# One-bank PSUM tiles for the last up projection of a fused attention and feed-forward kernel

## The chip, the cores and the metric

The kernel runs on one core of a Trainium2 chip. A core has TensorE (PE, matrix products, with a loader PEld for the stationary operand), VectorE (DVE), ScalarE (ACT), GpSimd (POOL) and the queue engine SyncE (SP). PSUM, where TensorE writes, is used here as eight banks of 128 partitions x 512 float32 values. The metric is the device time of one execution in microseconds (us); several runs are made, and the profile shows one execution.

## The reference

Two stages. A chunked linear attention with a decay per head, over 4 batches, 8 heads, 768 positions and 64 dimensions:

```python
for b in range(nb):
    intra = np.einsum('bhic,bhjc->bhij', qb, kb) * Dmask[None]
    intra = np.einsum('bhij,bhjd->bhid', intra, vb)
    inter = np.einsum('bhid,bhde->bhie', qb * lam_pow[None], kv_state)
    out[:, :, sl] = intra + inter
    kv_state = lam_block * kv_state + np.einsum('bhsd,bhse->bhde', kb * rev_pow[None], vb)
```

Its output, as 3072 tokens of 512 values, goes through a feed-forward layer of width 2048 with a leaky activation:

```python
h = x @ w_in
g = np.maximum(h, 0.0) + alpha * np.minimum(h, 0.0)
return g @ w_out
```

## The kernel before, in words

**Chunks.** The 3072 tokens are six chunks of 512. For each chunk the attention fills `XT[c]` (512 features x 512 tokens, transposed) in four groups (units, two batches x two halves of the heads). Then `up` makes 16 blocks f of 128 hidden features: four matmuls of 512 columns into one PSUM bank, a Relu on ACT (line 643, into a tile `m`), and one DVE operation (line 650) that puts the activated block g into SBUF. `down` multiplies the g blocks by `w_out`. The program order is written by hand (`manual_schedule`): every engine works through its instructions in the order in which the code issues them, and semaphores for data and buffers are put in by the framework.

**An attention group.** `cluster(old, new)` issues, for the unit `old`, `inter` (line 442) and `intra` (line 506) into the tile `acc`, and ACT's copy of `acc` into `XT` (line 298); for `new` the scores into the tile `s` (line 460 or 472), the mask on DVE (line 485 or 487) and the state products. `acc` and `s` are tiles of two banks each. The other four banks are two of the tag `h`, one `op` and one `tk`.

**Chunk 4.** A table `plan[4]` issues work ahead of numbered places x of an order of "U" (an up product of chunk 4) and "D" (a down product of chunk 3). There are 30 places, 0 to 29; the 15th and 16th U (`u` 14 and 15) stand at 27 and 29. The last attention groups, the sums of weights (`up_weight_add`, additions by DMA issued on POOL, line 716) and of the inputs (`up_x_sum`, lines 730 and 733) are hung on these places.

**The last up projection, fast products.** For chunk 5 the up projection pairs block f with block f+8 and uses seven half-size products in place of eight (Strassen's scheme, in Winograd's form). A pair has two banks, x and y, each cut into two halves (x0, x1, y0, y1), and `up_pair(f, stage, banks)` issues four stages:

- S f.1: products 1 and 5 into y0 and y1 (two matmuls of 256 columns each); ACT copies -y1 to SBUF (line 764, tile p) and -y0 into x0 (line 765).
- S f.2: products 2 and 6 into x0 and y0; DVE writes x1 = p - y0 (line 769).
- S f.3: products 7 and 3 into y0 and x1; DVE writes y1 = y0 - p (line 773).
- S f.4: product 4 into y0.

Then x holds block f and y block f+8. R is the Relu of one block on ACT (line 791), G the DVE operation that makes g (line 796). The list `LAST_UP` holds the order of this stretch: S, R and G as above; D i.b.part, four matmuls of 256 columns of chunk 4's down projection (line 854; it uses fast products too, i being the product); E i, the evacuation of the down product i (line 886 on ACT or 889 on DVE); Z and Y, sums of g blocks of chunk 4 or 5 on POOL (suffix G) or DVE (suffix V), line 837. U f is a plain up product of chunk 5 (`up_plain`, line 779) with its Relu. Pairs take their banks in turn from the tile `s`, the tile `acc`, and two `h` banks.

**The end.** `down2_last` issues the down projection of chunk 5: seven products x two halves of tokens, eight matmuls of 256 columns each, the first of which needs the blocks g 0 to 7.

Of the kernel before, what the change touches and what calls it, by code (L numbers as in the profile page):

```python
# [11 lines left out]
def kernel(  # L12
# [46 lines left out]
    o_pool = ctx.enter_context(tc.tile_pool(name="o", bufs=3))  # L59
    ps = ctx.enter_context(tc.tile_pool(name="ps", bufs=1, space=bass.MemoryType.PSUM))  # L60
    h_ps_pool = ctx.enter_context(tc.tile_pool(name="hps", bufs=2, space=bass.MemoryType.PSUM))

    lam_sb = const.tile([H, 1], fp32, name="lam_sb")
    nc.scalar.dma_start(out=lam_sb, in_=lam.rearrange("(h o) -> h o", o=1))
# [67 lines left out]

    zeros = const.tile([128, W], fp16, name="zeros")
    nc.vector.memset(zeros, 0.0)
    acc = ps.tile([128, 2, 512], fp32, tag="acc", name="acc")
    nc.vector.memset(acc[:, :, 256:512], 0.0)
    ident = const.tile([128, 128], fp16, name="ident")
    make_identity(nc, ident)
# [311 lines left out]

    def score_products(n):
        t = T[n]
        t["s"] = ps.tile([128, 2, 2, 2, L], fp32, tag="s", name="s")
        if units[n][0] >= HC:
            s = t["s"].rearrange("p l h x j -> p l h (x j)")
            for hp in range(2):
                for f in range(2):
                    for a, hl in QUADS:
                        p = ds(hl * 64, 64)
                        nc.tensor.matmul(  # L460
                            s[ds(a * 64, 64), hl, hp, ds(L * f, L - 64 * f)].rearrange("p (e j) -> p e j", e=2),
                            lhsT=t["qkT"][p, 1, f, hp, ds(a * 64, 64)],
                            rhs=t["qkT"][p, 0, :, hp, ds(a * 64 + 32 * f, 64 - 32 * f)],
                            start=True,
                            stop=True,
                        )
            return
        for hp in range(2):
            for e in range(2):
                for a, hl in QUADS:  # L470
                    p = ds(hl * 64, 64)
                    nc.tensor.matmul(  # L472
                        t["s"][ds(a * 64, 64), hl, hp, 1 - e, :].rearrange("p (e j) -> p e j", e=2),
                        lhsT=t["qkT"][p, 1, e, hp, ds(a * 64, 64)],
                        rhs=t["qkT"][p, 0, :, hp, ds(a * 64, 64)],
                        start=True,
                        stop=True,
                    )
# [147 lines left out]
    def g_of(c, f):  # L626
        half, f = divmod(f, NF // 2)
        return group_of(c, f // 2)[:, half, f % 2]

    def up(c, f, bi=None, bank="h"):  # L630
        h_ps = bank_of(bank, "h_ps")
        n = CH if bi is None else W
        for gi in range(NHP):
            x = XT[c][:, gi]
            nc.tensor.matmul(  # L635
                h_ps[:, 0:n] if bi is None else h_ps[:, 0:n].rearrange("p (e j) -> p e j", e=2),
                lhsT=w_in_sb[:, gi, ts(f, 128)],
                rhs=x.rearrange("p e b j -> p (e b j)") if bi is None else x[:, :, bi, :],
                start=(gi == 0),
                stop=(gi == NHP - 1),  # L640
            )
        m = m_pool.tile([128, CH], fp32, tag="m", name="m")
        nc.scalar.activation(m[:, 0:n], h_ps[:, 0:n], AF.Relu, scale=-1.0)  # L643
        g = g_of(c, f)
        if bi is None:
            g, mv, hv = g.rearrange("p e b j -> p (e b j)"), m, h_ps
        else:
            g = g[:, :, bi, :]
            mv, hv = (y[:, 0:n].rearrange("p (e j) -> p e j", e=2) for y in (m, h_ps))
        nc.vector.scalar_tensor_tensor(  # L650
            out=g, in0=mv, scalar=oma[:, f : f + 1], in1=hv, op0=ALU.mult, op1=ALU.add
        )
# [121 lines left out]
        else:  # L774
            up_product(4, f, y0, False)

    def up_plain(f, bank):
        for g in range(NHP):
            nc.tensor.matmul(  # L779
                bank,  # L780
                lhsT=w_in_sb[:, g, ts(f, 128)],
                rhs=XT[NC - 1][:, g].rearrange("p e b j -> p (e b j)"),
                start=(g == 0),
                stop=(g == NHP - 1),
            )
        P[f] = bank
        up_relu(f)

    def up_relu(f):
        m = m_pool.tile([128, CH], fp32, tag="m", name="m")  # L790
        nc.scalar.activation(m, P[f], AF.Relu, scale=-1.0)  # L791
        P[f] = (m, P[f])
# [101 lines left out]
    def down2(c, x):  # L894
# [8 lines left out]
            evacuated(c, i, t)  # L903

    LAST_UP = """
        U0 D1.0.0 G0 U8 G8 S1.1 S3.1 S2.1 D1.0.1 D1.1.0 D1.1.1 S1.2 S3.2 S2.2 D2.0.0 Z2.0G S1.3 R1
        S3.3 S2.3 S1.4 D2.0.1 D2.1.0 E1 S3.4 Z2.3G G1 D2.1.1 Z2.1G Z2.2V D6.0.0 R9 R11 G9 R2 R3 E2
        G11 D6.0.1 S4.1 S2.4 R10 G3 Z4.3G D6.1.0 Z4.1G D6.1.1 S6.1 G2 S4.2 D5.0.0 E6 D5.0.1 D5.1.0
        G10 S4.3 S6.2 S5.1 Z4.2V D5.1.1 S4.4 R12 R4 S6.3 D7.0.0 G12 E5 Z4.0G S5.2 D7.0.1 D7.1.0
        S6.4 G4 R6 S7.1 S5.3 D7.1.1 D3.0.0 R5 Y0G G6 S5.4 Y1G R14 R13 E7 S7.2 D3.0.1 D3.1.0 D3.1.1  # L910
        G5 G13 S7.3 R7 D4.0.0 G14 D4.0.1 D4.1.0 S7.4 D4.1.1 Y2G R15 G7 E3 G15 Y3V E4
    """.split()

    def last_up(c):

        sets = [ps.tile([128, 2, CH], fp32, tag=tag, name="up_ps") for tag in ("s", "acc")]
        sets = [(t[:, 0], t[:, 1]) for t in sets]
        banks = {}
        plain = [int(t[1:]) for t in LAST_UP if t[0] == "U"]
        for t in LAST_UP:  # L920
            kind, x = t[0], t[1:].rstrip("VG").split(".")
            eng, x = t[-1], [int(y) for y in x]
            if kind == "U":
                up_plain(x[0], sets[plain.index(x[0])][0])
            elif kind == "S":
                f, stage = x
                if stage == 1:
                    at = (f - len(plain) // 2) % 3
                    banks[f] = sets[at] if at < 2 else (bank_of("h", "up_x"), bank_of("h", "up_y"))
                    P[f], P[f + NF // 2] = banks[f]  # L930
                up_pair(f, stage, banks[f])
            elif kind == "R":
                up_relu(x[0])
            elif kind == "G":
                up_g(x[0])
            elif kind == "D":
                i, b, part = x
                side = dict(CHAIN)[i]
                if (b, part) == (0, 0) and i in (1, 2, 5):
                    O[c, side] = bank_of("op" if side == 0 else "tk", "o_ps")  # L940
                product(
                    c, i, b, O[c, side], (b, part) == (0, 0) and i in (1, 2, 5), i in (2, 3, 4) and (b, part) == (1, 1),
                    ds(256 * b, 256), fs=range(4 * part, 4 * part + 4),
                )
            elif kind == "E":
                evacuated(c, x[0], O[c, dict(CHAIN)[x[0]]])
            elif kind == "Z":
                g_sum(c, x[0], x[1], eng)
            elif kind == "Y":
                sums13(c + 1, x[0], eng)  # L950

    def down2_last(c):
# [3 lines left out]
        for i, side, b in order:  # L956
            if i in (1, 2):
                O[c, side, b] = bank_of({(1, 0): "tk", (1, 1): "op"}.get((side, b), "h"), "o_ps")
            t = O[c, side, b]
            if (i, b) == (4, 1):  # L960
                for x, bank in enumerate(("s", "acc")):
                    p4 = ps.tile([128, 2, CH], fp32, tag=bank, name="p4")[:, 0]
                    product(c, i, b, p4, True, True, ds(0, 128), ds(128 * x, 128))
                    o = O[c, "out"]["c21"][:, b, ds(128 * x, 128)]
                    nc.vector.tensor_tensor(out=o, in0=o, in1=p4[:, 0:128], op=ALU.add)
                    write(c, 1, 0, o, b, ds(128 * x, 128), nc.scalar)
                continue
            product(c, i, b, t, i in (1, 2, 5), i in (2, 3, 4), ds(0, 256))
            evacuated(c, i, t[:, 0:256], b)
            if (i, b) == (7, 1):  # L970
                evacuated(c, None, t[:, 0:256], b)
            if i == 1:
                for j in range(4):
                    g_sum(c, 2, j, "V", b)
            if i == 2 and b == 1:
                for j in range(4):
                    g_sum(c, 4, j, "V")
# [315 lines left out]
    def turned(n):  # L1293
# [30 lines left out]
            10: lambda: (up_weight_add(1), up_weight_add(3)),  # L1324
            14: lambda: (cluster(21, 22), up_weight_add(2)),
            22: lambda: cluster(22, 23),
            24: lambda: (up_weight_add(4), up_x_tiles()),
            26: lambda: (up_x_sum(0), up_x_sum(1)),
            28: lambda: cluster(23, None),
            29: lambda: (up_x_sum(2), up_x_sum(3), up_x_sum(4)),  # L1330
        },
    }
    order = {c: "U" + "DU" * 9 + "U" + "DU" * 5 for c in plan}
# [7 lines left out]
    for c, at in plan.items():  # L1341
        u = d = w = 0
        for x, what in enumerate(order[c]):
            if x in at:
                at[x]()
            if what == "U":
                up(c, u // 2 + 8 * (u % 2), None, "h")
                u += 1
                if u in (10, 12, 14, 16):
                    sums13(c, u // 2 - 5)  # L1350
# [46 lines left out]
```

## Time and profile before

| What | Value |
|---|---|
| Median of 3 runs | 207.98 us (207.56 to 208.16) |
| Time of the profiled execution | 207.6 us |
| Its span, first to last instruction | 205.8 us |
| TensorE busy | 198.7 us (97%) |
| VectorE busy | 160.8 us (78%) |
| ScalarE busy | 118.0 us (57%) |
| GpSimd busy | 125.2 us (61%) |
| Granted TensorE clock | 1.00 |
| `LAST_UP` on TensorE | 162.60 to 189.77 |

How to read the lines: in the waits, an engine and line, what it waited for, total us, number of times and the longest. In the timeline, start, duration, engine, line of the kernel, operation, output<-inputs, shape, how many instructions are merged, and in brackets the idle time of the engine just before, with what ended it. Rows on PE end when the last result has left; the next matmul starts before that. In a row of a stretch: start and end, length, busy us (instructions) of PE, PEld, DVE, ACT and POOL, granted clock, share of the transfers' engines, GB/s. In a row of a tile: minimum, median and maximum duration in ns.

### The profile page before, as it was taken

The numbers are of one execution on the slowest core, as the hardware profiler recorded it, in microseconds if no ns is written. First come the engines' busy times: TensorE is split into PE (matmuls) and PEld (weight loads), VectorE is DVE, ScalarE is ACT, GpSimd is POOL, SyncE is SP. The second block draws the span as 40 slices with busy tenths as digits, with TensorE's granted clock in tenths as the row PEclk, the third lists the DMA queues.
The fourth block names the chain that finished last, engine by engine and source line by source line (L and its number), as shares of the span: only waits on it lengthen the run. The fifth ranks groups of instructions, "written<-read, shape, count | busy, mean of one in ns | idle before, by whom it ended". The sixth has DMA issues, their size and how long they took to land.

```text
span 205.8 us, 5753 instructions
## 1 busy us (share of the span) xinstructions
PE 198.7 (97%) x2313; PEld 125.2 (61%) x2313; DVE 160.8 (78%) x301; ACT 118.0 (57%) x227; POOL 125.2 (61%) x151
## 2 busy tenths in 40 slices
PE   7999999999999999999999999999999999989993
PEld 6776445556445455555555455467767578878783
DVE  6978879567889747899996879959888747876941
ACT  7985778144776217656776466643544656564220
POOL 8999894053469883296497677967295074754000
PEclk9999999999999999999999999999999999999999
DMA  5999999997999997899999984299956200101223
GB/s 162 279 197 234 247 264 207 234 288 229 222 231 283 201 262 155 219 179 168 258 167 211 224 161 79 47 233 346 210 107 153 102 5 0 53 3 53 102 86 121
DMA packets 65536, 35.91 MB, mean 174 GB/s; under 512 B 33685, under 2 KB 61477, under 8 KB 65509
## 3 DMA queue, kind: packets, MB, share of 16 engines
q1 hardware_dynamic: 47124, 23.74, 49.6%
q0 software_dynamic: 18080, 11.67, 36.0%
q8 instruction: 18, 0.29, 0.6%
q10 hardware_dynamic: 304, 0.13, 0.2%
q14 instruction: 10, 0.07, 0.1%
HBM read 27.27 MB, written 6.29 MB: 163 GB/s over the span
## 4 chain that ended last, share of the span: by engine, by line
PE 89%; DVE 5%; ACT 3%; issue 1%; ACTq 0%
PE h_ps L635 34%; PE o_ps L663 21%; PE o_ps L854 16%; PE up_ps L747 3%; PE s L472 3%; PE acc L506 3%; PE acc L442 2%; ACT m L791 2%; PE tpx L408 2%; DVE g L796 1%; DVE dmask L212 1%; PE acc L526 1%; PE up_ps L779 1%; ACT L190 1%; ACT xT L298 1%
## 5 line engine op out<-in xcount | busy, mean ns | idle before, releaser
L635 PE MATMUL h_ps<-xT,w_in_sb 128*128 128x512 f16 (+1 forms) x328 | 75.9, 374 | 0.0
L650 DVE SCALAR_TENSOR_TENSOR g<-m,oma,h_ps 128x512 f16<-128x512 f32 (+1 forms) x82 | 59.2, 732 | 16.5 <-ACT m L643 13.5
L643 ACT ACTIVATE m<-h_ps 128x512 f32<-128x512 f32 (+1 forms) x82 | 47.7, 586 | 33.0 <-PE h_ps L635 27.7
L635 PEld LDWEIGHTS <-w_in_sb 128*128 128x128 f16 x328 | 31.2, 98 | 32.5
L663 PE MATMUL o_ps<-w_out_sb,g 128*128 128x512 f16 x192 | 46.8, 380 | 0.0
L487 DVE TENSOR_TENSOR sm<-s,dmask 128x1024 f16<-128x1024 f32 x20 | 24.4, 1220 | 11.3 <-PE s L472 11.2
L854 PEld LDWEIGHTS <-g 128*128 128x128 f16 x296 | 28.0, 98 | 6.3 <-DVE g L796 0.6
L663 PEld LDWEIGHTS <-g 128*128 128x128 f16 x192 | 17.6, 98 | 19.4 <-DVE g L650 0.2
L298 ACT ACTIVATE xT<-acc 128x512 f16<-128x512 f32 x24 | 14.3, 597 | 23.7 <-PE acc L526 21.5
L422 POOL TENSOR_TENSOR qdT<-qkT,qdecay 128x512 f16<-128x512 f16 (+1 forms) x19 | 21.4, 1132 | 5.4 <-DMA qkT<-qk 5.4
L854 PE MATMUL o_ps<-w_out_sb,g 128*128 128x256 f16 x192 | 24.4, 273 | 0.3 <-DVE g L796 0.3
L837 POOL TENSOR_TENSOR s<-g 128x512 f16<-128x512 f16 x11 | 13.6, 1240 | 14.4 <-DVE g L650 8.1
L358 POOL TENSOR_TENSOR kdec<-kraw,kdecay 128x512 f16<-128x512 f32 x14 | 14.9, 1074 | 5.9 <-DMA kraw<-in_k_dram 5.9
L837 POOL TENSOR_TENSOR g<-g 128x512 f16<-128x512 f16 x14 | 16.1, 1160 | 3.5 <-PE o_ps L854 2.6
L302 POOL CAST qk<-qraw 128x512 f16<-128x512 f32 x12 | 7.8, 652 | 15.9 <-DMA qraw<-in_q_dram 15.0
L555 DVE SCALAR_TENSOR_TENSOR R<-R,rdecay,acc 128x128 f16<-128x128 f16 x54 | 15.5, 340 | 0.1
L344 POOL DMA_DIRECT2D v<-in_v_dram x15 | 11.7, 792 | 0.5 <-issue 0.4
L791 ACT ACTIVATE m<-up_ps 128x512 f32<-128x512 f32 x12 | 7.1, 598 | 7.7 <-DVE up_ps L773 5.3
L886 ACT ACTIVATE o_sb<-o_ps 128x512 f32<-128x512 f32 (+1 forms) x15 | 7.5, 498 | 6.9 <-PE o_ps L854 4.7
L854 PE MATMUL o_ps<-w_sum,g 128*128 128x256 f16 x88 | 11.2, 273 | 0.0
L796 DVE SCALAR_TENSOR_TENSOR g<-m,oma,up_ps 128x512 f16<-128x512 f32 x12 | 8.8, 744 | 2.9 <-ACT m L791 2.4
L302 POOL CAST qk<-kraw 128x512 f16<-128x512 f32 x9 | 5.5, 611 | 7.9 <-DMA kraw<-in_k_dram 7.9
(129 smaller groups left out, 281.7 us busy)
## 6 DMA issues: line engine op xcount, KB each, us to landing
out_dram<-o_sb SPq DMA_DIRECT2D x20, 256.0 KB, 2.6
qraw<-in_q_dram SPq DMA_DIRECT2D x6, 512.0 KB, 5.7
kraw<-in_k_dram SPq DMA_DIRECT2D x5, 512.0 KB
w_in_sb<-in_moe_w_in_dram POOLq DMA_DIRECT2D x4, 512.0 KB, 7.9
w_out_sb<-in_moe_w_out_dram POOLq DMA_DIRECT2D x4, 512.0 KB, 10.5
wi_sum<-w_in_sb SPq DMA_DIRECT2D x4, 512.0 KB, 4.8
v<-in_v_dram POOLq DMA_DIRECT2D x15, 128.0 KB, 5.1
qraw<-in_q_dram POOLq DMA_DIRECT2D x6, 256.0 KB, 7.0
```

What stands on the lines that cost most here:

```text
L298: nc.scalar.activation(out, in_, AF.Copy)
L302: nc.gpsimd.tensor_copy(out=out, in_=in_)
L358: engine(eng).tensor_tensor(out=kdec, in0=kr, in1=decay[:, ds(4 * hh, 4), :].rearrange("p h e -> p e h").unsqueeze(3).to_broadcast([128, 2 ...
L422: engine(eng).tensor_tensor(out=qdT[:, :, :, p], in0=(t["qps"] if eng == "P" else t["qkT"][:, 0])[:, :, :, p], in1=qdecay[:, hh, :, :, p], ...
L487: nc.vector.tensor_tensor(out=t["sm"].rearrange("p a h x j -> p (a h) x j"), in0=t["s"].rearrange("p a h x j -> p (a h) x j"), in1=mask_of ...
L555: nc.vector.scalar_tensor_tensor(out=R[b, hh, m + 1][:, hp], in0=R[b, hh, m][:, hp], scalar=rdecay[:, 2 * hh + hp : 2 * hh + hp + 1], in1= ...
L635: nc.tensor.matmul(h_ps[:, 0:n] if bi is None else h_ps[:, 0:n].rearrange("p (e j) -> p e j", e=2), lhsT=w_in_sb[:, gi, ts(f, 128)], rhs=x ...
L643: nc.scalar.activation(m[:, 0:n], h_ps[:, 0:n], AF.Relu, scale=-1.0)
L650: nc.vector.scalar_tensor_tensor(out=g, in0=mv, scalar=oma[:, f : f + 1], in1=hv, op0=ALU.mult, op1=ALU.add)
L663: nc.tensor.matmul(o_ps, lhsT=lhs(c, f, t), rhs=w_out_sb[:, f, :], start=(f == 0), stop=(f == NF - 1),)
L837: engine(eng).tensor_tensor(out=out, in0=in0, in1=in1, op=op)
L854: nc.tensor.matmul(t[:, cols], lhsT=x, rhs=w, start=(fresh and f == fs[0]), stop=(last and f == fs[-1]), skip_group_check=True,)
```

## The change

The tiles `acc` and `s` move from the pool `ps` into a pool of their own. That pool is closed after the last attention group, and a new pool takes its four banks as four tiles of one bank each, `up0` to `up3` (`spare`). The pairs of `LAST_UP` use `spare[2:4]`, `spare[0:2]` and two `h` banks in turn. The two plain products U0 and U8 become an eighth pair (f = 0). The last attention group, with the closing of the pool, moves from place 28 to 26 of chunk 4, and three other items of the plan one or two places sooner. The 15th and 16th up product of chunk 4 go into `up2` and `up0` in place of `h` banks. The order in `LAST_UP` is a new one. The last two products of the kernel use `spare[0]` and `spare[2]`.

```diff
+    attention = ExitStack()
+    att_pool = attention.enter_context(tc.tile_pool(name="att", bufs=1, space=bass.MemoryType.PSUM))
...
-    acc = ps.tile([128, 2, 512], fp32, tag="acc", name="acc")
+    acc = att_pool.tile([128, 2, 512], fp32, tag="acc", name="acc")
...
-        t["s"] = ps.tile([128, 2, 2, 2, L], fp32, tag="s", name="s")
+        t["s"] = att_pool.tile([128, 2, 2, 2, L], fp32, tag="s", name="s")
...
+    spare = []
+
     def up(c, f, bi=None, bank="h"):
-        h_ps = bank_of(bank, "h_ps")
+        h_ps = spare[bank] if isinstance(bank, int) else bank_of(bank, "h_ps")
...
     LAST_UP = """
-        U0 D1.0.0 G0 U8 G8 S1.1 S3.1 S2.1 D1.0.1 D1.1.0 D1.1.1 S1.2 S3.2 S2.2 D2.0.0 Z2.0G S1.3 R1
-        S3.3 S2.3 S1.4 D2.0.1 D2.1.0 E1 S3.4 Z2.3G G1 D2.1.1 Z2.1G Z2.2V D6.0.0 R9 R11 G9 R2 R3 E2
-        G11 D6.0.1 S4.1 S2.4 R10 G3 Z4.3G D6.1.0 Z4.1G D6.1.1 S6.1 G2 S4.2 D5.0.0 E6 D5.0.1 D5.1.0
-        G10 S4.3 S6.2 S5.1 Z4.2V D5.1.1 S4.4 R12 R4 S6.3 D7.0.0 G12 E5 Z4.0G S5.2 D7.0.1 D7.1.0
-        S6.4 G4 R6 S7.1 S5.3 D7.1.1 D3.0.0 R5 Y0G G6 S5.4 Y1G R14 R13 E7 S7.2 D3.0.1 D3.1.0 D3.1.1
-        G5 G13 S7.3 R7 D4.0.0 G14 D4.0.1 D4.1.0 S7.4 D4.1.1 Y2G R15 G7 E3 G15 Y3V E4
+        S0.1 S1.1 S2.1 D1.0.0 S0.2 D1.0.1 D1.1.0 S1.2 S0.3 R0 S2.2 D1.1.1 S0.4 R8 G0 Z2.0G Z2.1G
+        S1.3 R1 S2.3 G8 D2.0.0 S1.4 R9 G1 E1 D2.0.1 D2.1.0 Z2.2G S3.1 S2.4 R10 D2.1.1 D6.0.0 G9
+        Z2.3V S4.1 R2 E2 S3.2 Z4.2G G10 D6.0.1 D6.1.0 D6.1.1 S3.3 G2 D5.0.0 D5.0.1 R3 S3.4 R11 G3
+        Z4.3G S4.2 S5.1 D5.1.0 D5.1.1 G11 Z4.1G S4.3 E6 S6.1 S5.2 Y1G S4.4 R12 Z4.0G D7.0.0 E5 R4
+        D7.0.1 G12 S6.2 G4 D7.1.0 D7.1.1 S7.1 E7 S5.3 Y0G S6.3 D3.0.0 S7.2 R5 S5.4 R6 R13 G6
+        D3.0.1 D3.1.0 G5 G13 S7.3 D3.1.1 R7 G7 S6.4 D4.0.0 D4.0.1 D4.1.0 R14 S7.4 R15 G14 Y2G
+        D4.1.1 E3 G15 Y3V E4
     """.split()

+    def open_spare():
+
+        attention.close()
+        pool = ctx.enter_context(tc.tile_pool(name="last", bufs=1, space=bass.MemoryType.PSUM))
+        for x in range(4):
+            spare.append(pool.tile([128, CH], fp32, tag=f"up{x}", name=f"up{x}"))
...
-        sets = [ps.tile([128, 2, CH], fp32, tag=tag, name="up_ps") for tag in ("s", "acc")]
-        sets = [(t[:, 0], t[:, 1]) for t in sets]
+        sets = [spare[2:4], spare[0:2]]
...
-                    at = (f - len(plain) // 2) % 3
+                    at = f % 3
...
-                for x, bank in enumerate(("s", "acc")):
-                    p4 = ps.tile([128, 2, CH], fp32, tag=bank, name="p4")[:, 0]
+                for x in range(2):
+                    p4 = spare[2 * x]
...
-            24: lambda: (up_weight_add(4), up_x_tiles()),
-            26: lambda: (up_x_sum(0), up_x_sum(1)),
-            28: lambda: cluster(23, None),
-            29: lambda: (up_x_sum(2), up_x_sum(3), up_x_sum(4)),
+            23: lambda: (up_weight_add(4), up_x_tiles()),
+            24: lambda: (up_x_sum(0), up_x_sum(1)),
+            26: lambda: (cluster(23, None), open_spare()),
+            28: lambda: (up_x_sum(2), up_x_sum(3), up_x_sum(4)),
...
-                up(c, u // 2 + 8 * (u % 2), None, "h")
+                up(c, u // 2 + 8 * (u % 2), None, {(4, 14): 2, (4, 15): 0}.get((c, u), "h"))
```

More of the change, by code (lines that the diff above doesn't have):

```diff
@@ L775, in up_pair @@
             up_product(4, f, y0, False)
[L777 to L787, printed above, removed]
     def up_relu(f):
@@ L905 @@
     LAST_UP = """
-        U0 D1.0.0 G0 U8 G8 S1.1 S3.1 S2.1 D1.0.1 D1.1.0 D1.1.1 S1.2 S3.2 S2.2 D2.0.0 Z2.0G S1.3 R1
-        S3.3 S2.3 S1.4 D2.0.1 D2.1.0 E1 S3.4 Z2.3G G1 D2.1.1 Z2.1G Z2.2V D6.0.0 R9 R11 G9 R2 R3 E2
-        G11 D6.0.1 S4.1 S2.4 R10 G3 Z4.3G D6.1.0 Z4.1G D6.1.1 S6.1 G2 S4.2 D5.0.0 E6 D5.0.1 D5.1.0
-        G10 S4.3 S6.2 S5.1 Z4.2V D5.1.1 S4.4 R12 R4 S6.3 D7.0.0 G12 E5 Z4.0G S5.2 D7.0.1 D7.1.0
-        S6.4 G4 R6 S7.1 S5.3 D7.1.1 D3.0.0 R5 Y0G G6 S5.4 Y1G R14 R13 E7 S7.2 D3.0.1 D3.1.0 D3.1.1
-        G5 G13 S7.3 R7 D4.0.0 G14 D4.0.1 D4.1.0 S7.4 D4.1.1 Y2G R15 G7 E3 G15 Y3V E4
-    """.split()
+        S0.1 S1.1 S2.1 D1.0.0 S0.2 D1.0.1 D1.1.0 S1.2 S0.3 R0 S2.2 D1.1.1 S0.4 R8 G0 Z2.0G Z2.1G
[5 more added lines that the diff above has]
+        D4.1.1 E3 G15 Y3V E4
+    """.split()
+    def open_spare():
[3 more added lines that the diff above has]
+            spare.append(pool.tile([128, CH], fp32, tag=f"up{x}", name=f"up{x}"))
     def last_up(c):
-        sets = [ps.tile([128, 2, CH], fp32, tag=tag, name="up_ps") for tag in ("s", "acc")]
-        sets = [(t[:, 0], t[:, 1]) for t in sets]
+        sets = [spare[2:4], spare[0:2]]
         banks = {}
-        plain = [int(t[1:]) for t in LAST_UP if t[0] == "U"]
         for t in LAST_UP:
@@ L922, in last_up @@
             eng, x = t[-1], [int(y) for y in x]
-            if kind == "U":
-                up_plain(x[0], sets[plain.index(x[0])][0])
-            elif kind == "S":
+            if kind == "S":
                 f, stage = x
                 if stage == 1:
-                    at = (f - len(plain) // 2) % 3
+                    at = f % 3
                     banks[f] = sets[at] if at < 2 else (bank_of("h", "up_x"), bank_of("h", "up_y"))
```

## The prediction

> **What bounds the kernel now.** I read the page first, then the busy time by stretch and the waits of TensorE in the last stretch, then the timeline around each of them.
>
> ```profile
> PE 198.7 (97%) x2313; PEld 125.2 (61%) x2313; DVE 160.8 (78%) x301; ACT 118.0 (57%) x227; POOL 125.2 (61%) x151
> ...
> 162.60:189.77 27.17, 25.59 (x220) 21.23 (x218) 18.93 (x34) 15.30 (x34) 15.36 (x14) 1.00 0.09 31
> ...
> PEld L747 <- issue: 2.6, 5, 0.8
> ...
> PE up_ps L747 <- DVE g L796: 1.0, 3, 0.6
> PE up_ps L747 <- ACT m L791: 0.6, 2, 0.3
> ```
>
> TensorE is the bound, so only its waits and its own work count. The stretch row is the last chunk's up projection (`LAST_UP`): the granted clock is 1.00 and transfers have a share of 0.09. The waits (total us, times, longest) lie in it: five before the products of line 747. They understate the loss, since a matmul's shown end reaches past the moment at which the next could have started, so I count matmuls against starts.
>
> ```profile
> 161.74 1.03 PE L635 MATMUL h_ps<-xT,w_in_sb 128*128 128x512 f16 x4
> 162.60 1.03 PE L779 MATMUL up_ps<-xT,w_in_sb 128*128 128x512 f16 x4
> ...
> 189.77 0.93 PE L854 MATMUL o_ps<-w_out_sb,g 128*128 128x256 f16 x7
> ...
> 191.03 10.76 PE o_ps L854 x97
> ...
> 201.63 1.06 PE L854 MATMUL p<-w_sum,g 128*128 128x128 f16 x16
> ```
>
> Four 512-wide matmuls take 162.60 - 161.74 = 0.86, or 0.215 each; 97 matmuls of 256 columns take 201.63 - 191.03 = 10.60, or 0.1093 each. `LAST_UP` before holds 8 wide ones (U0, U8), 7 pairs x 14 and 7 down products x 16 narrow ones: 8 x 0.215 + 210 x 0.1093 = 24.67. It takes 189.77 - 162.60 = 27.17, so 2.50 are lost to waits. Behind it seven matmuls of the last chunk run to 189.77 + 7 x 0.1093 = 190.54 and the eighth starts at 191.03: 0.49 more. After that TensorE runs to its end without a gap (the x97 row).
>
> **Why it waits.** Four of these stalls, each with its releaser:
>
> ```profile
> 164.30 0.75 DVE L796 SCALAR_TENSOR_TENSOR g<-m,oma,up_ps 128x512 f16<-128x512 f32 x1
> 165.10 0.38 PE L747 MATMUL up_ps<-x_neg,w_in_sb 128*128 128x256 f16 x2 [0.17 <-DVE g L796]
> ...
> 170.10 0.38 PE L747 MATMUL up_ps<-xT,wi_sum 128*128 128x256 f16 x2
> 170.52 0.43 DVE L773 TENSOR_TENSOR up_ps<-up_ps,p 128x256 f32<-128x256 f32 x1 [0.37 <-PE up_ps L747]
> 170.54 0.38 PE L747 MATMUL up_x<-xT,wi_sum 128*128 128x256 f16 x2
> 170.86 0.42 DVE L773 TENSOR_TENSOR up_y<-up_y,p 128x256 f32<-128x256 f32 x1
> 170.98 0.38 PE L747 MATMUL up_ps<-xT,wi_sum 128*128 128x256 f16 x2
> 170.99 0.60 ACT L791 ACTIVATE m<-up_ps 128x512 f32<-128x512 f32 x1 [3.18 <-DVE up_ps L773]
> 171.64 0.38 PE L747 MATMUL up_ps<-x_sum,w_in_sb 128*128 128x256 f16 x2 [0.28 <-ACT m L791]
> ...
> 182.36 0.74 DVE L796 SCALAR_TENSOR_TENSOR g<-m,oma,up_ps 128x512 f16<-128x512 f32 x1
> 183.16 0.38 PE L747 MATMUL up_ps<-x_neg,w_in_sb 128*128 128x256 f16 x2 [0.58 <-DVE g L796]
> ...
> 189.59 0.60 ACT L791 ACTIVATE m<-up_ps 128x512 f32<-128x512 f32 x1 [0.53 <-PE up_ps L747]
> 190.22 0.75 DVE L796 SCALAR_TENSOR_TENSOR g<-m,oma,up_ps 128x512 f16<-128x512 f32 x1 [1.20 <-ACT m L791]
> ```
>
> At 165.10 S1.1 writes the second bank (y) of the pair `s`. Only G0 (DVE to 165.05) holds it up, and G0 reads U0 in the first bank. At 171.64 S1.4 writes y again and waits for R1 (ACT to 171.59), which reads x; R1 itself waited for line 773, which writes y. At 183.16 S7.1 waits for G4, again the other bank. At 190.22 G7 (x) waits for R15 (y), and the last chunk's eighth matmul needs G7. None of these pairs shares a bank. They share a tile of two banks, and the waits follow the tile. The pair f=3 lies in two one-bank tiles (`up_x`, `up_y`): its line 773 starts at 170.86, while the matmul into `up_x` runs to 170.92; in the two-bank tile line 773 starts at 170.52, only after the matmul into the other bank (to 170.48). So with one-bank tiles these waits should go.
>
> **The change, part by part.** *One-bank tiles* take away the cause of the waits: up to 2.50 + 0.49. *The eighth pair* replaces 8 wide matmuls by 14 narrow ones: 8 x 0.215 - 14 x 0.1093 = 1.72 - 1.53 = 0.19 less on TensorE. It adds four instructions, one of each of these rows:
>
> ```profile
> L764 ACT ACTIVATE p<-up_ps x5: 383/383/384, 165.7 to 183.8; 128x256 f32<-128x256 f32 x5
> L765 ACT ACTIVATE up_ps<-up_ps x5: 368/368/368, 166.1 to 184.2; 128x256 f32<-128x256 f32 x5
> L769 DVE TENSOR_TENSOR up_ps<-p,up_ps x5: 420/429/430, 168.8 to 186.3; 128x256 f32<-128x256 f32 x5
> L773 DVE TENSOR_TENSOR up_ps<-up_ps,p x5: 433/433/433, 170.5 to 187.9; 128x256 f32<-128x256 f32 x5
> ```
>
> That is 0.75 on ACT and 0.86 on DVE. From the stretch row ACT goes to 15.30 + 0.75 = 16.1 and DVE to 18.93 + 0.86 = 19.8, against 224 x 0.1093 = 24.48 of TensorE: covered on average; it costs something only where a handoff is late (below). The re-laid stretch also moves two of the sums (Z) from DVE to POOL and one back.
>
> The Trainium skill ("TensorE: Matmul & The Clock Gate", Back-to-back issue gap) speaks against this part: it gives a sustained 131 ns for 512 columns and 81 ns for 128, by which the eighth pair would cost at least 14 x 81 - 8 x 131 = 86 ns where I have a gain, and the whole gain would be an estimated 0.28 smaller. The rows above show 215 ns here, so I keep the 0.19.
>
> *The attention group two places sooner* moves line 442 and 506's matmuls (and ACT's copy) ahead of one down product and one up product, and moves no DMA. The weight sum issued one place sooner stands between the same two neighbours on POOL's queue.
>
> ```profile
> 155.60 0.95 DVE L485 TENSOR_TENSOR sm<-s,dmask 128x768 f16<-128x768 f32 x1
> ...
> 158.70 0.60 ACT L643 ACTIVATE m<-h_ps 128x512 f32<-128x512 f32 x1 [1.14 <-PE h_ps L635]
> ...
> 160.24 0.39 PE L442 MATMUL acc<-qdT,R 128*128 128x128 f16 x4
> 160.56 0.37 PE L506 MATMUL acc<-sm,v 64*64 64x128 f16 x16
> 160.98 0.60 ACT L298 ACTIVATE xT<-acc 128x512 f16<-128x512 f32 x1
> 162.40 0.42 DVE L733 TENSOR_TENSOR x_sum<-xT,x_sum 128x512 f16<-128x512 f16 x1
> ```
>
> The group occupies 160.24 to 160.85 on TensorE and now starts two products (1.73) sooner, at 158.50; its input, line 485, is done at 156.55. Same matmuls, so 0 on TensorE. What it buys is that the four banks are free: the 15th up product goes into `up2` at 159.98 (one down product, 0.87, behind the group at 159.11), and if the reopened pool waits for everything of the old one, that is line 298's copy: behind the previous Relu (from 158.70, 0.60) it runs 159.30 to 159.90. Slack 0.08; all of TensorE's work is queued behind it, and should the copy start a Relu later it is a wait of 0.5. The sums of the inputs move with the group (line 733, 0.42 each, and one on ACT): the last three follow the 15th product's G on DVE and end near 163.5, the first of them read at 164.35 by S0.2; nothing waits.
>
> *The new order* I laid out by hand on the old clock: TensorE back to back from 162.60 (stages 1 to 3 and a D part 0.437, stage 4 0.219), the other engines in program order, with the durations of the rows above (Relu 0.60, G 0.75), 0.04 for a handoff and 0.27 from a narrow matmul's start to its end (0.38 for two, less 0.109). Queued behind one another, Relus start 0.47 apart and G's 0.65:
>
> ```profile
> 173.40 0.59 ACT L791 ACTIVATE m<-up_y 128x512 f32<-128x512 f32 x1
> ...
> 173.87 0.60 ACT L791 ACTIVATE m<-up_ps 128x512 f32<-128x512 f32 x1
> ...
> 174.80 0.74 DVE L796 SCALAR_TENSOR_TENSOR g<-m,oma,up_y 128x512 f16<-128x512 f32 x1
> ...
> 175.45 0.74 DVE L796 SCALAR_TENSOR_TENSOR g<-m,oma,up_x 128x512 f16<-128x512 f32 x1
> ```
>
> An item waits for its own bank alone. The tightest:
>
> ```
> TensorE item   would start   needs                           ready    slack
> S0.2           164.35        x0 of S0.1 (ACT)                164.16   0.19
> S0.3 (p. 3)    166.32        w4 sum landed                   163.0    3.3
> S0.4           167.40        line 773 of S0.3 (DVE)          167.22   0.18
> S1.4           168.93        line 773 of S1.3 (behind G0)    168.76   0.17
> S3.1           170.02        G8 (behind S1.3, S2.3)          169.75   0.27
> D6.0.1         172.42        Z2.3V                           171.5    0.9
> S6.1           177.44        G11                             177.0    0.4
> S7.2           182.46        x0 of S7.1 (ACT, behind G4)     182.05   0.4
> S7.3           183.98        line 769 of S7.2                183.5    0.5
> S7.4           186.38        line 773 of S7.3 (behind G13)   185.9    0.5
> last chunk f=7 187.79        G7                              186.5    1.3
> ```
>
> The w4 sum is the one transfer with a new deadline, and the last chunk's half sums are the DVE work just behind:
>
> ```profile
> 153.97 0.86 POOL L716 DMA_DIRECT2D wi_sum<-wi_sum  x1
> ...
> DMA to landing us min/median/max: 4.4/5.0/9.0
> ...
> 193.13 1.70 DVE L837 TENSOR_TENSOR g<-s,g 128x256 f16<-128x256 f16 x8
> ```
>
> Even the slowest landing gives 153.97 + 9.0 = 163.0. On DVE G15 and then Y3V end near 189.4 and the first four half sums take 0.85 (half of the x8 row), to 190.3; the product that reads them begins at 187.03 + 4 x 0.874 = 190.5: no new wait there.
>
> **Sum.** `LAST_UP`: 27.17 to 24.48, so -2.69 (2.50 waits, 0.19 work); eighth matmul: -0.49; four handoffs under 0.2 of slack: between 0 and four stalls of 0.44 (the size of those at 166 to 186: 171.64 - (170.98 + 2 x 0.109)), so 0 to +1.8; I take +0.15, near nothing, since each has slack on the rows' own durations. Net -3.03. The profiled execution is 205.8 of span and 1.8 around it, 207.6: it would be 204.6. It stands 0.38 under the median of the runs, 207.98, so the median would be 204.95. I say **204.9**.
>
> **Rivals.** *The new order gives part back.* The early part is densest: G0, G8 and four of lines 769 and 773 follow one another on DVE from 166.4 to 169.8. For it: four slacks of 0.2 or less. Against it: slack grows to 0.4 and more later. Three stalls of 0.44 make 1.3: 206.2.
>
> *The waits stay*, because the reopened banks are still tracked together. Then in the new order S1.1 waits for the G of the 16th up product (162.60 + 0.17 + 0.60 + 0.75 and three handoffs: 164.2 for 163.04, so 1.2), S0.4, S1.4 and S3.4 each for a Relu of the other bank (0.44), S7.1 for G4 (181.2 for 180.71: 0.5): 1.2 + 3 x 0.44 + 0.5 = 3.0 of the 3.18 come back, 207.8. Against it: the `up_x` rows.
>
> *Slower: ACT blocked at S7.1.* Its copy into x0 waits for G4, G4 for R4, R4 stands behind E5, which waits for D5.1.1; behind the copy wait R5, R6, R13, R7, so G6 to G7, S7.3, and the last chunk's first product. The copy has 0.4 of slack; what G4 is late beyond that is added to the end. To end 0.8 slower than before (208.8) the copy must end 3.0 + 0.4 + 0.8 = 4.2 late, at 186.3. The longest wait of ACT before line 791 is 3.18 (the row at 170.99), and that one waited for a bank it does not share. Unlikely.
>
> **How the numbers follow.** Forecast (204.9) 0.72, order gives part back (206.2) 0.16, waits stay (207.8) 0.07, slower (208.8) 0.05. This kernel's runs can tell 0.3% (0.62 us) from no change: faster 0.89 (the first two and a hundredth of the third), within 0.06, slower 0.05. The range leaves the last two out: from 204.2 (the lowest run shown, 207.56, less 3.18, is 204.4, and 0.2 for scatter) to 206.6 (three stalls and the 0.38 of the median).
>
> **What would show it.** Right: no wait of TensorE on line 796 or 791 in the last stretch; the Relu of an x bank starting before line 773's end on its y bank; the last chunk's products starting 2.7 sooner and the x97-like run of them without a gap; one pair more and no line 779. Wrong: waits before S0.4, S1.4 or S3.1 named by line 769, 773 or 796 (first rival); an up product waiting at the reopened bank for longer than 0.3; a wait for G of the other bank (second); ACT's line 765 idle for microseconds at S7.1 (third). The forecast fails if TensorE's loss between the first pair and its end is over 1.5.

## The result, and the profile after

The changed kernel's median is 204.43 us (203.99 to 204.76, 5 runs), beside 207.63 (207.56 to 208.16, 5 runs) of the kernel before in the same comparison: a ratio of 0.9837, 95% interval 0.9815 to 0.9859. The profiled execution has a span of 203.0 in place of 205.8. The forecast was 204.9, with a range of 204.2 to 206.6.

The page's engine line, the row of the stretch `LAST_UP` in a table of busy time by stretch (same columns as before), and the run of matmuls behind it in the chain of waits, all of the changed kernel:

```profile
PE 197.8 (97%) x2319; PEld 126.8 (62%) x2319; DVE 161.6 (80%) x302; ACT 118.5 (58%) x229; POOL 125.5 (62%) x152
...
162.95:187.40 24.45, 24.45 (x225) 21.91 (x224) 19.20 (x38) 15.70 (x36) 16.05 (x15) 1.00 0.10 35
...
187.13 11.79 PE o_ps L846 x108
```

The stretch takes 24.45 in place of 27.17, and TensorE is busy for all of it. From the first pair to the kernel's last product there is not one wait of TensorE. The last chunk's first product starts at 187.40 and the final one of 128 columns at 198.76: 11.36, where before 189.77 to 201.63 took 11.86. So the stretch gives 2.72 and its successor 0.50. Ahead of the stretch 0.35 is lost (162.95 in place of 162.60); the experiments come back to that.

The same handoffs in the timeline of the changed kernel (lines 773 and 777 are the old 769 and 773, 783 the Relu, 788 the G):

```profile
159.59 0.60 ACT L300 ACTIVATE xT<-acc 128x512 f16<-128x512 f32 x1
160.35 1.03 PE L639 MATMUL up<-xT,w_in_sb 128*128 128x512 f16 x4
162.95 0.38 PE L751 MATMUL up<-x_neg,w_in_sb 128*128 128x256 f16 x2
...
167.04 0.43 DVE L777 TENSOR_TENSOR up<-up,p 128x256 f32<-128x256 f32 x1
167.08 0.60 ACT L783 ACTIVATE m<-up 128x512 f32<-128x512 f32 x1 [1.58 <-PE up L751]
167.75 0.38 PE L751 MATMUL up<-x_sum,w_in_sb 128*128 128x256 f16 x2
168.58 0.43 DVE L777 TENSOR_TENSOR up<-up,p 128x256 f32<-128x256 f32 x1
169.28 0.38 PE L751 MATMUL up<-x_sum,w_in_sb 128*128 128x256 f16 x2
...
187.40 3.66 PE L846 MATMUL o_ps<-w_out_sb,g 128*128 128x256 f16 x32
```

The Relu R0 reads the x bank from 167.08 while line 777 still writes the y bank (167.04 to 167.47), which no pair of the kernel before does. S0.4 starts at 167.75, 0.28 after line 777; S1.4 at 169.28, 0.27 after the next line 777 (to 169.01). The 15th up product starts at 160.35, 0.16 after the attention's copy (to 160.19).

The Trainium skill ("PSUM — Partial Sum Buffer", PSUM bank collisions raise a hardware error) asks for semaphores by bank and quadrant; banks of one tile need none between them by that rule. The overlap of R0 and line 777, 167.08 against 167.04 to 167.47, agrees.

### The profile page after: what moved, and what is told of

It reads as the page before. It is cut to its first block, busy times and chain, and to the rows that moved or that the text cites. A ratio compares the mean times of both kernels' runs of the same rounds, so it can differ in the third digit from the quotient of the medians.

```text
span 203.0 us, 5771 instructions
## 1 busy us (share of the span) xinstructions
PE 197.8 (97%) x2319; PEld 126.8 (62%) x2319; DVE 161.6 (80%) x302; ACT 118.5 (58%) x229; POOL 125.5 (62%) x152
## 4 chain that ended last, share of the span: by engine, by line
PE 90%; DVE 6%; ACT 2%; issue 0%; ACTq 0%
PE h_ps L639 32%; PE o_ps L667 21%; PE o_ps L846 16%; PE up L751 5%; PE s L474 3%; PE acc L508 3%; PE acc L444 2%; PE tpx L410 2%; DVE dmask L214 1%; PE acc L528 1%; PE up_y L751 1%; DVE g L654 1%; DVE g L829 1%; PE up L639 1%; ACT L192 1%; ACT xT L300 1%
## 5 line engine op out<-in xcount | busy, mean ns | idle before, releaser
L639 PE MATMUL h_ps<-xT,w_in_sb 128*128 128x512 f16 (+1 forms) x320 | 74.0, 374 | 0.2 <-DVE g L654 0.2
L654 DVE SCALAR_TENSOR_TENSOR g<-m,oma,h_ps 128x512 f16<-128x512 f32 (+1 forms) x80 | 57.7, 732 | 13.8 <-ACT m L647 11.1
L647 ACT ACTIVATE m<-h_ps 128x512 f32<-128x512 f32 (+1 forms) x80 | 46.6, 586 | 31.6 <-PE h_ps L639 28.6
L829 POOL TENSOR_TENSOR g<-g 128x512 f16<-128x512 f16 x15 | 17.3, 1164 | 2.0 <-PE o_ps L846 1.2
L783 ACT ACTIVATE m<-up 128x512 f32<-128x512 f32 x12 | 7.1, 597 | 5.9 <-PE up L751 5.8
L881 DVE TENSOR_TENSOR o_sb<-o_sb,o_ps 128x512 f32<-128x512 f32 (+1 forms) x12 | 6.5, 550 | 4.4 <-PE o_ps L846 2.2
```

What stands on the lines that cost most here:

```text
L639: nc.tensor.matmul(h_ps[:, 0:n] if bi is None else h_ps[:, 0:n].rearrange("p (e j) -> p e j", e=2), lhsT=w_in_sb[:, gi, ts(f, 128)], rhs=x ...
L654: nc.vector.scalar_tensor_tensor(out=g, in0=mv, scalar=oma[:, f : f + 1], in1=hv, op0=ALU.mult, op1=ALU.add)
L829: engine(eng).tensor_tensor(out=out, in0=in0, in1=in1, op=op)
```

## The experiments

Three theories stood against each other. **A**: the waits come from tiles of two banks, and one-bank tiles remove them. **B**: the new order removes them. **C**: the early attention group and the reopened banks for the 15th and 16th up product are needed. The kernel before was timed again in two further comparisons, on two chips: 207.33 (7 runs) beside e1, e2, e3 and e4, 207.66 (17 runs) beside the others. Each ratio is to the kernel before of the same comparison; the changed kernel was not timed again beside e1 to e4.

| Run | Tiles | Order | Pair f=0 | Median, us | Ratio to before (95%) | `LAST_UP` on TensorE, us |
|---|---|---|---|---|---|---|
| before (first comparison) | two banks | old | plain | 207.63 | | 27.17 |
| changed | one | new | fast | 204.43 | 0.9837 (0.9815 to 0.9859) | 24.45 |
| e1 | two | new | fast | 210.76 | 1.0161 (1.0146 to 1.0176) | 30.79 |
| e2 | one | old | plain | 204.47 | 0.9859 (0.9841 to 0.9878) | 24.65 |
| e3 | one | new | plain | 204.75 | 0.9879 (0.9856 to 0.9903) | 24.65 |
| e4 | one, late group | new | fast | 204.61 | 0.9865 (0.9847 to 0.9883) | 24.45 |
| e4b | as e4, bank filled | new | fast | 205.36 | 0.9891 (0.9871 to 0.9910) | 24.45 |
| e5 | two, G7 first | old | plain | 207.12 | 0.9978 (0.9968 to 0.9987) | 27.15 |
| e6 | one, sums apart | new | fast | 204.32 | 0.9841 (0.9825 to 0.9857) | 24.45 |
| e7 | the changed kernel again | new | fast | 204.22 | 0.9842 (0.9823 to 0.9861) | 24.45 |

### e1: two-bank tiles in the new order

```diff
-        for x in range(4):
-            spare.append(pool.tile([128, CH], fp32, tag=f"up{x}", name=f"up{x}"))
+        for x in range(2):
+            two = pool.tile([128, 2, CH], fp32, tag=f"up{x}", name=f"up{x}")
+            spare.extend([two[:, 0], two[:, 1]])
```

> The changed kernel, but the reopened pool holds two tiles of two banks in place of four of one; order, eighth pair and early group stay. Theory A (waits follow the tile): the waits come back in the new order, at S1.1 (about 1.2, for the G of the 16th up product), S0.4, S1.4 and S3.4 (about 0.44 each, for a Relu of the other bank) and S7.1 (0.5): about 3 us, so 207.4 to 207.8. Theory B (the new order is what removed the waits): no such waits, 204.4.

Measured: 210.76, 3.4 slower than the kernel before. In the traces the stretch takes 30.79 where the changed kernel's takes 24.45, 6.3 more. A holds in kind, B falls: the waits are back with the tiles alone. But the expected 3 us was half of it. The waits of TensorE and of its loader in this kernel, and from its timeline one chain and the waits of S7.1 and S7.4:

```profile
PE up L751 <- DVE g L788: 2.2, 2, 1.3
PE up L751 <- ACT m L783: 1.7, 3, 1.1
PE up L751 <- DVE g L654: 1.0, 1, 1.0
...
PEld L751 <- issue: 6.4, 8, 1.5
```

```profile
169.39 0.60 ACT L783 ACTIVATE m<-up 128x512 f32<-128x512 f32 x1 [0.47 <-PE up L751]
170.02 0.75 DVE L788 SCALAR_TENSOR_TENSOR g<-m,oma,up 128x512 f16<-128x512 f32 x1 [1.22 <-ACT m L783]
170.69 0.42 DVE L777 TENSOR_TENSOR up<-up,p 128x256 f32<-128x256 f32 x1
...
171.15 0.60 ACT L783 ACTIVATE m<-up 128x512 f32<-128x512 f32 x1 [1.16 <-DVE up L777]
171.79 0.38 PE L751 MATMUL up<-x_sum,w_in_sb 128*128 128x256 f16 x2 [1.13 <-ACT m L783]
...
185.97 0.38 PE L751 MATMUL up<-x_neg,w_in_sb 128*128 128x256 f16 x2 [1.29 <-DVE g L788]
...
192.68 0.38 PE L751 MATMUL up<-x_sum,w_in_sb 128*128 128x256 f16 x2 [0.88 <-DVE g L788]
```

R8 (y bank, 169.39) holds up G0 (x bank, 170.02). Behind G0 on DVE's queue stands line 777 of the *next* pair (170.69), R1 on ACT (171.15) waits for that, and S1.4 waits for R1: one false wait is passed on through two queues to another tile. My 3 us had counted each TensorE item against its own tile only.

Counted from start to start, as in the prediction, three of its five waits came at their price: S1.1 lost 1.19, S0.4 0.44 and S3.4 0.45. The other two came at about three times theirs, S1.4 at 1.29 and S7.1 at 1.46. S7.4 (1.04, behind a G) and two smaller ones at S4.3 and S6.1 (0.22 each) were not on the list. Together these make the 6.3.

### e2: one-bank tiles in the old order

```diff
+    attention = ExitStack()
+    att_pool = attention.enter_context(tc.tile_pool(name="att", bufs=1, space=bass.MemoryType.PSUM))
...
-            28: lambda: cluster(23, None),
+            28: lambda: (cluster(23, None), open_spare()),
...
-        sets = [ps.tile([128, 2, CH], fp32, tag=tag, name="up_ps") for tag in ("s", "acc")]
-        sets = [(t[:, 0], t[:, 1]) for t in sets]
+        sets = [spare[2:4], spare[0:2]]
```

> The kernel before, with only the tiles changed: the attention's pool is closed after the last group where it stands, and the pairs use four one-bank tiles; old order, U0 and U8 plain, group and inputs at their old places. Theory A: all waits of the stretch go, 2.50 + 0.49, so 207.6 - 3.0 = 204.6. Theory B: the old order still waits, 207 or more. Theory C (early group and spare banks are needed): something near 206.

Measured: 204.47, as theory A expected, and not to be told from the changed kernel by the time. No wait of TensorE is left in the stretch; it runs from 162.45 to 187.10, 24.65, where the count of its matmuls gave 24.67. The end of it, where before G7 waited for R15:

```profile
186.66 0.74 DVE L799 SCALAR_TENSOR_TENSOR g<-m,oma,up 128x512 f16<-128x512 f32 x1
186.66 0.60 PE L857 MATMUL o_ps<-w_sum,g 128*128 128x256 f16 x4
186.91 0.60 ACT L794 ACTIVATE m<-up 128x512 f32<-128x512 f32 x1 [0.98 <-PE up L750]
187.10 3.66 PE L857 MATMUL o_ps<-w_out_sb,g 128*128 128x256 f16 x32
```

G7 (186.66) now starts ahead of R15 (186.91). B and C both fall: neither the order nor the early group is needed for the gain. The pool is closed and reopened in e1 too, and there the waits are back; so it is the split into one-bank tiles, not the new pool, that removes them.

### e3: the pair f=0 as two plain products

```diff
-        S0.1 S1.1 S2.1 D1.0.0 S0.2 D1.0.1 D1.1.0 S1.2 S0.3 R0 S2.2 D1.1.1 S0.4 R8 G0 ...
+        U0 S1.1 S2.1 D1.0.0 U8 D1.0.1 D1.1.0 S1.2 R0 S2.2 D1.1.1 R8 G0 ...
```

> The changed kernel with U0 and U8 as plain products (8 matmuls of 512 columns) in place of the eighth pair, in one-bank tiles, rest of the order unchanged. Theory A: 0.19 of TensorE work comes back and nothing waits, 204.6. Rival: the wider products cost nothing or gain, because the pair's two ACT and two DVE operations cost more than it saves: 204.3 or less. The trace shows the work exactly: 24.67 from the first U to the last chunk's first product, where the changed kernel has 24.45.

Measured: 204.75, and a stretch of 24.65 beside 24.45:

```profile
162.67:187.32 24.65, 24.65 (x220) 21.32 (x219) 18.33 (x36) 15.21 (x34) 16.20 (x15) 1.00 0.11 34
```

The trace shows 0.20 for the 0.19 expected. The medians lean the same way, but their intervals overlap, so the time alone does not show it. DVE has 0.87 less here (18.33 for 19.20) and ACT 0.49 less; the difference costs the changed kernel nothing. The Trainium skill's 131 ns for 512 columns ("TensorE: Matmul & The Clock Gate", Back-to-back issue gap) is not met here, where the four of U0 take 162.67 to 163.53, 0.215 each: by the 131 ns this kernel's stretch would be the shorter one.

### e4 and e4b: the group at its old place

```diff
-            26: lambda: (cluster(23, None), open_spare()),
-            28: lambda: (up_x_sum(2), up_x_sum(3), up_x_sum(4)),
+            28: lambda: (cluster(23, None), open_spare()),
+            29: lambda: (up_x_sum(2), up_x_sum(3), up_x_sum(4)),
...
-                up(c, u // 2 + 8 * (u % 2), None, {(4, 14): 2, (4, 15): 0}.get((c, u), "h"))
+                up(c, u // 2 + 8 * (u % 2), None, {(4, 15): 0}.get((c, u), "h"))
```

> The changed kernel with the last attention group, the reopening of the banks and the last input sums at their old places (28 and 29); the 15th up product uses an h bank again, the 16th the reopened bank. Theory A: the move only frees banks and brings nothing by itself; 204.4, no new wait over 0.2. Theory C: the early group is needed, with waits at S0.2 for the input sums or at the 16th up product for the attention's copy: 0.5 to 1.5 more, 205 to 206.

Measured: 204.61, with no wait of TensorE in the stretch: theory A. In this kernel nothing fills the bank `up2` before the pair f=0 adds into it, so products 2 and 3 of that pair overwrite in part and the kernel does not compute the whole sum; the instructions are as many and as long (the stretch is 24.45 again), so the time can be compared. By the Trainium skill ("PSUM — Partial Sum Buffer", The four PSUM rules) a matmul that does not open a group adds only where a matmul has written since the bank's marks were last cleared, and overwrites elsewhere; no run here times that. e4b fills the bank with one matmul of 512 columns right behind the reopening:

```diff
-            28: lambda: (cluster(23, None), open_spare()),
+            28: lambda: (cluster(23, None), open_spare(), cover(spare[2])),
```

> The late group again (group, reopening and last input sums at their old places), with one 512-column matmul into up2 just after the reopening. In the late group without it, nothing had filled that bank before the pair f=0 accumulates into it, so its products 2 and 3 overwrote there in part; the instructions and their lengths were the same. Theory A: 0.22 of TensorE more and no wait, 204.7; the early place of the group is there so that the 15th and 16th up product cover the two x banks and brings no time beyond that 0.2. Theory C: a wait at the reopened bank, 205 or more.

Measured: 205.36, where theory A expected 204.7: theory C's wait at the reopened bank is there. The covering matmul waits:

```profile
161.02 0.60 ACT L300 ACTIVATE xT<-acc 128x512 f16<-128x512 f32 x1
161.67 0.38 PE L916 MATMUL up<-ident 128*128 128x512 f16 x1 [0.70 <-ACT xT L300]
```

It writes `up2`, which lies where the scores were (`s`), and `s` was last read five microseconds earlier (by the mask, line 487, to 156.66). Yet it waits 0.70 for ACT's copy out of `acc`: here the first use of the reopened pool waited for the last work on the closed one, in another tile. That is the wait the prediction guarded against. In the changed kernel one down product (0.87) lies between the group and the 15th up product, which starts 0.16 after the copy, so the wait is covered, if narrowly. So the early group does buy something for the eighth pair: the 15th and 16th up products fill its x bank and the next pair's without an extra matmul and without this wait. The kernel of e2 has no need of that, since there U0 and U8 fill them.

### e5: one false wait undone in the kernel before

```diff
-        G5 G13 S7.3 R7 D4.0.0 G14 D4.0.1 D4.1.0 S7.4 D4.1.1 Y2G R15 G7 E3 G15 Y3V E4
+        G5 G13 S7.3 R7 D4.0.0 G14 D4.0.1 D4.1.0 S7.4 D4.1.1 Y2G G7 R15 E3 G15 Y3V E4
```

> The kernel before with one swap at the end of the stretch: G7 is issued ahead of R15. The two-bank tiles stay. Theory A: G7 then waits only for S7.4's matmuls (end 189.50) and ends at about 190.3, ahead of 190.54 when the last chunk's eighth matmul needs it; R15 and G15 come after it and are needed later. The 0.49 of the last wait goes and the other 2.5 stay: 206.9 to 207.1 beside 207.4. If the 0.49 was not the wait of G7 for R15, nothing changes.

Measured: 207.12 beside 207.66, a ratio of 0.9978 (0.9968 to 0.9987): 0.54 less, for 0.49 expected. In the trace the last chunk, from its first product to its final one, takes 11.36 in place of 11.86. The two-bank tiles are still there:

```profile
189.51 0.38 PE L747 MATMUL up_ps<-x_sum,w_in_sb 128*128 128x256 f16 x2
190.00 0.75 DVE L796 SCALAR_TENSOR_TENSOR g<-m,oma,up_ps 128x512 f16<-128x512 f32 x1 [0.58 <-PE up_ps L747]
190.16 3.66 PE L854 MATMUL o_ps<-w_out_sb,g 128*128 128x256 f16 x32
190.78 0.60 ACT L791 ACTIVATE m<-up_ps 128x512 f32<-128x512 f32 x1 [1.32 <-DVE g L796]
```

Now G7 (x) waits for S7.4's matmuls (y, to 189.89), and R15 (y) waits for G7 (x): the false wait is turned around, and the last chunk runs 32 matmuls without a gap. The 0.49 term and the reading of that wait both hold.

### e6 and e7: what is lost ahead of the stretch

In the changed kernel's profiled execution an up product of chunk 4 waits at 151.85, an instruction that the change does not touch. On POOL, DVE and TensorE:

```profile
148.77 0.90 POOL L720 DMA_DIRECT2D wi_sum<-wi_sum  x1 [5.19 <-DMA wi_sum<-w_in_sb]
149.40 1.45 POOL L829 TENSOR_TENSOR s<-g 128x512 f16<-128x512 f16 x1
...
149.56 1.59 DVE L829 TENSOR_TENSOR g<-g 128x512 f16<-128x512 f16 x1
150.62 1.03 PE L639 MATMUL h_ps<-xT,w_in_sb 128*128 128x512 f16 x4
151.07 0.73 DVE L654 SCALAR_TENSOR_TENSOR g<-m,oma,h_ps 128x512 f16<-128x512 f32 x1
...
151.85 1.02 PE L639 MATMUL h_ps<-xT,w_in_sb 128*128 128x512 f16 x4 [0.20 <-DVE g L654]
```

POOL's sum starts late because a transfer landed late. DVE's sum of two SBUF inputs, 0.42 when alone, then takes 1.59 beside it, and the G behind it is late for a bank: 151.85 in place of 151.48 (0.86 behind 150.62), 0.37. In the kernel before TensorE did not wait there:

```profile
148.10 0.90 POOL L716 DMA_DIRECT2D wi_sum<-wi_sum  x1 [4.20 <-DMA wi_sum<-w_in_sb]
148.74 1.45 POOL L837 TENSOR_TENSOR s<-g 128x512 f16<-128x512 f16 x1
...
149.57 0.91 DVE L837 TENSOR_TENSOR g<-g 128x512 f16<-128x512 f16 x1
```

Nor did it in a second profiled execution of the changed kernel (e7), where the transfer landed sooner:

```profile
147.99 0.90 POOL L720 DMA_DIRECT2D wi_sum<-wi_sum  x1 [4.36 <-DMA wi_sum<-w_in_sb]
148.62 1.45 POOL L829 TENSOR_TENSOR s<-g 128x512 f16<-128x512 f16 x1
...
149.30 1.07 DVE L829 TENSOR_TENSOR g<-g 128x512 f16<-128x512 f16 x1
```

The Trainium skill ("SBUF — State Buffer", Who interferes with whom) has a rule for it: a DVE instruction with two SBUF inputs contends with a GpSimd instruction that reads SBUF. The trace agrees, with 1.59 for 0.42. e6 moves four of these sums on DVE ahead of POOL's:

```diff
-    for x in range(4):
-        sums_at[4][13 + 2 * x] = (4, x, "V")
+    for x, place in enumerate((9, 11, 13, 13.5)):
+        sums_at[4][place] = (4, x, "V")
```

> The changed kernel with four sums of chunk 3 on DVE (line 829 with suffix V, places 13, 15, 17, 19 of chunk 4) moved to 9, 11, 13 and 13.5, ahead of the moment when POOL starts its own sums. In the changed kernel one of them took 1.59 beside POOL's sum, in place of 0.42, and an up product waited 0.36 for the G behind it. If that is what the executions differ in ahead of the stretch: sums of 0.42 to 0.5, no wait there, 204.1 to 204.3 and less spread. Rival: the sums now delay the attention's mask or G at 143 to 148, and a wait appears there: 204.6 or more.

> The changed kernel once more, on the same chip as the three others: 204.4 by its runs so far, with a wait ahead of the stretch of 0 to 0.5 that differs from execution to execution and the stretch itself at 24.45.

Measured: e6 204.32 (204.09 to 204.40, 4 runs), e7 204.22 (203.98 to 204.77, 4 runs). The sums of e6 do run alone:

```profile
143.37 0.42 DVE L829 TENSOR_TENSOR g<-g 128x512 f16<-128x512 f16 x1
145.44 0.42 DVE L829 TENSOR_TENSOR g<-g 128x512 f16<-128x512 f16 x1
147.17 0.75 DVE L829 TENSOR_TENSOR g<-g 128x512 f16<-128x512 f16 x2
```

and TensorE has no wait from 20 us on. But e7's profiled execution has none there either: its stretch begins at 162.33, e6's at 162.58. The median did not move, so e6 beats nothing; that its runs lie closer together (0.31 for 0.79) rests on four runs each and stays open. The 0.25 between the two starts is older than these sums: the matmuls of line 410 that start at 24.30 in e7 start at 24.55 in e6. It arises in the first 24 us; what causes it there stays open.

## Why the prediction was right

**The reading of the waits** held. That waits follow the tile, not the bank, was read from five pairs of rows; e1 and e2 show it from both sides, each with the order and the work held fixed.

**The sum.** The stretch was to go from 27.17 to 24.48 and went to 24.45; the eighth matmul was to start without its 0.49 and does. The eighth pair's 0.19 shows as 24.65 against 24.45 (e3). The term that was mis-sized is the allowance of +0.15 for late handoffs: none was late. The slacks were 0.28 (S0.4), 0.27 (S1.4) and 0.16 (the 15th up product), each about 0.1 more than laid out; an engine two or three tenths later at one of them would have used it up. In the profiled execution the 0.37 of the unrelated wait took the place of the allowance; without the one and the other the sum gives 207.6 - 3.18 = 204.4. The forecast of 204.6 for the profiled execution, which took 204.73, was close partly by luck: one loss that was allowed for did not come, and another that was not foreseen did. The step from one execution to the median (0.38 added) was too much: further runs of the kernel before lowered its median from 207.98 to 207.63, and 207.63 - 3.18 is 204.45. That this meets the measured 204.43 so closely is chance, as the five runs lie 0.8 apart.

**The rivals.** "The new order gives part back" did not occur. "The waits stay" was priced wrong, and in sign: e1, which is that case, is 3.4 slower than before, not 0.2 faster. Its list of waits (3.0) left out that a false wait on one tile delays what stands behind it on DVE and ACT for other tiles: S1.4 and S7.1 cost three times their price there, and S7.4 was not listed. The forecast's margin thus hung on the tiles more than I had said: without them this order is worse than the old one, and the slower side of the chances belonged there. The rival that had it, ACT blocked at S7.1, did not occur: in the changed kernel no wait showed at S7.1.

**The order and the early group** were costed at nothing, and the time shows no gain from them beside the tiles: e2 has neither and the same time within its interval. The early group only spares the eighth pair the wait of e4b.

## What to carry to other kernels

Where instructions on different banks wait for one another, look at how the banks were allocated before re-ordering anything: a tile of two banks was tracked as one. Splitting it in the old order alone gave 2.9 us of the 3.2 that the whole change gave, and 0.2 of the rest is the eighth pair. A false wait can cost more than its own length, when it holds up the queues of the engines that serve other tiles; an order laid out for independent banks took 6.3 us longer when they were not. Put other work between the closing of a pool and the first use of its memory, because the first use can wait for work on the old pool's other tiles, 0.70 in e4b.

## What the runs showed of the hardware

The same DVE sum of two SBUF inputs took 0.42 alone and 0.91 to 1.59 beside a POOL sum in the rows above, and how long they met went with when an unrelated transfer landed: in two executions of the changed kernel POOL waited 4.36 and 5.19 for it, and the DVE sum took 1.07 and 1.59. Only the second cost TensorE anything, 0.37. I had not expected a scatter of some tenths of a microsecond to come from there. e6 removes the meeting, though not visibly from the time.
